# Expert matmuls over 240 instead of 256 token columns in a retention, mixture-of-experts and MLP kernel

## The chip, the core and the metric

The kernel runs on one core of one Trainium2 chip, as one program. The metric is the device time of an execution in microseconds (us); lower is better. Five engines work side by side and wait for each other through semaphores: TensorE (PE in the profile; its weight loads are listed apart as PEld), VectorE (DVE), ScalarE (ACT), GpSimd (POOL) and SyncE (SP), which here only issues DMAs. SBUF is the on-chip memory that the engines read; PSUM is the memory into which matmuls accumulate.

## What is computed

A retention layer (attention with a decay per head), then a layer of 8 experts in which each token goes to the one expert with the largest gate logit, then a dense two-layer MLP. Cut to the shapes and the parts that matter here:

```python
# q, k, v: (2, 8, 768, 64), lam: (8,)
x = attn(q, k, v, lam)                     # -> (1536 tokens, 512)

# experts: w_gate (512, 8), w1 (8, 512, 1024), w2 (8, 1024, 512)
logits = x @ w_gate
expert_idx = np.argmax(logits, axis=1)
gate_w = softmax(logits)[np.arange(N), expert_idx]
for e in range(E):
    mask = expert_idx == e
    h = np.maximum(x[mask] @ w1[e], 0.0)
    out[mask] = gate_w[mask, None] * (h @ w2[e])

# second MLP: w_in (512, 2048), w_out (2048, 512)
h = out @ w_in
return (h - np.tanh(h)) @ w_out
```

With the reference's own inputs the eight experts get 195, 205, 194, 205, 168, 157, 227 and 185 tokens, counted from `expert_idx`.

## The kernel before

The program has three stages, and PE goes through them in an order that is written out by hand.

**Attention and routing** (0 to about 97 us of the profile). Twelve tiles of 128 tokens. Matmuls here are plain float32 (type `F32`). Each tile's tokens are scaled by their gate and scattered by expert into rows of the DRAM tensor `xs_d`. `finish_routing` (line 485) counts the tokens of each expert and sets the flag `over` if a count is larger than `CAP` (256).

**Experts** (about 97 to 289 us). All matmuls of this stage are of type `F32R`, in which a matmul is one weight load and one matmul record. To keep float32's precision, each operand is split in a high and a low `F32R` part (`split`, lines 147 to 153: an ACT copy makes the high part at line 151, a DVE subtraction the low part at line 152), and each product is made of three matmuls: high by high, low by high, high by low. The stage has 64 steps n (8 experts by 8 blocks of 128 hidden columns, `EF` = 8). A step's `e_first` (lines 584 to 604) makes 12 matmuls with `w1` as the stationary operand and the tokens of the expert as the moving one, over `CAP` = 256 columns of tokens, whatever the expert's count is; ACT's Relu (line 602) and a DVE operation (line 603) turn the result into the two parts of `hb`. `e_second` (lines 608 to 629), two steps later, makes 12 matmuls with `w2` as the stationary and `hb` as the moving operand, again over 256 columns, and sums the 8 blocks in the two PSUM banks of `yp`. After an expert's last block ACT (line 627) and DVE (line 629) copy `yp` into `ysort`, from the column where the expert's tokens start; the columns beyond its count are overwritten by the next expert's copy.

In the same steps SP loads the weights ahead (`e_load1` for step n + 4, `e_load2` for step n + 2, 256 KB each) and, every second step, 512 KB of the second MLP's weights, which arrive as float64 and are turned into float32 by ACT, DVE and POOL (`decode_load`, `decode_math`, `decode_end`, lines 113 to 142). The two buffers `raw` of these loads are freed by the DVE operation at line 132, and SP, which issues in order, waits for that before it issues what stands behind. `x_trans` (line 524) turns the next expert's tokens once in 8 steps, with 8 transposes on PE.

**Second MLP** (about 289 us to the end). `m_first` (line 842) and `m_second` (line 922), all `F32R`, over windows of 512, 512, 256 and 256 tokens.

If `over` is set, a general path runs behind all of this (`window_table`, `window`): it takes the experts in windows of 256 tokens, and then the second MLP once more.

Of the kernel before, what the change touches and what calls it, by code (L numbers as in the profile page):

```python
# [13 lines left out]
ALU = mybir.AluOpType  # L14
# [1 line left out]
PSUM = bass.MemoryType.PSUM  # L16
DRAM = bass.MemoryType.DRAM

# (1 - tanh(s)/s)/s^2 with u = s^2 on 0 <= u <= T2, as Q4*((u+A1)^2+B1)*((u+A2)^2+B2)
T2 = 0.36  # L20
Q4 = 0.006269319839325208
A1, B1 = 0.64716093, 2.51604722 ** 2
A2, B2 = -2.33084468, 1.56360238 ** 2
# [4 lines left out]
def retention_moe_mlp(ctx: ExitStack, tc: tile.TileContext, q, k, v, lam, w_gate, w1, w2, w_in, w_out, out):  # L28
    nc = tc.nc
    pe, act, dve, pool, sp = nc.tensor, nc.scalar, nc.vector, nc.gpsimd, nc.sync  # L30
# [9 lines left out]
    EF = F // 128  # L40
    NF = FF // 128
    CAP = 256

    const = ctx.enter_context(tc.tile_pool(name="const", bufs=1))
    small = ctx.enter_context(tc.tile_pool(name="small", bufs=2))
# [4 lines left out]
    def slot(shape, dtype, name):  # L50
        return slp.tile(shape, dtype, tag="sl", name=name)

    def bank(shape, name):
        return ps.tile(shape, F32, tag="ps", name=name)

    def sm(shape, dtype, name):
        return small.tile(shape, dtype, tag=name, name=name)
# [30 lines left out]
    over = const.tile([128, 1], I32, name="over")  # L88
# [5 lines left out]
    biass = const.tile([128, 1], F32, name="biass")  # L94
    ysort = const.tile([128, KD, NT + CAP], F32, name="ysort")

# [10 lines left out]
    rev = at.tile([128, H], F32, name="rev")  # L107
    state = [at.tile([128, HP, 128], F32, name=f"state{b}") for b in range(B)]

# [1 line left out]
    dec = {}  # L111

    def decode_load(i):
# [60 lines left out]
    def e_split(n, which, new=slot):  # L174
        ews[n, which] = split(ewr.pop((n, which)), f"w{which}", new)

# [1 line left out]
    qkv = {}  # L178

    qrows, qts, qds = {}, {}, {}  # L180
# [281 lines left out]
    def setup_late():  # L462
# [6 lines left out]
        dve.tensor_copy(out=ebase_b, in_=ebase_i)  # L469
        pool.iota(slots_i, pattern=[[1, CAP]], base=1, channel_multiplier=0)  # L470
        dve.tensor_copy(out=slots, in_=slots_i)
# [9 lines left out]
    ebase_i = const.tile([128, E], I32, name="ebase_i")  # L481
    slots_both = slot([128, 2, CAP], F32, "slots")
    slots, slots_i = slots_both[:, 0, :], slots_both[:, 1, :].bitcast(I32)

    def finish_routing():
        tp = bank([128, E], "tp")
        pe.matmul(tp, lhsT=ones_b, rhs=cnt, start=True, stop=True)
        dve.tensor_copy(out=ct, in_=tp)
        inc = sm([128, E], F32, "inc")
        dve.tensor_tensor_scan(out=inc, data0=ones[:, 0:E], data1=ct, initial=0.0, op0=ALU.mult, op1=ALU.add)  # L490
        dve.tensor_tensor(out=starts, in0=inc, in1=ct, op=ALU.subtract)
        dve.tensor_copy(out=starts_i, in_=starts)
        cm = sm([128, 1], F32, "cm")
        dve.tensor_reduce(out=cm, in_=ct, axis=AX.X, op=ALU.max)
        dve.tensor_scalar(out=over, in0=cm, scalar1=float(CAP), scalar2=None, op0=ALU.is_gt)

    def token_table():
        dl = sm([128, E], F32, "dl")
# [11 lines left out]
        else:  # L510
            pool.dma_start(out=idx, in_=tok_d.rearrange("(t p) o -> p (t o)", p=128))

# [1 line left out]
    xrow, xhl = {}, {}  # L514

    def x_load(e):
# [7 lines left out]
    def x_trans(e):  # L524
        r = xrow.pop(e)
        hs, ls = [], []
        for g in range(2):
            xp = bank([128, 2, 2, 128], "xtp")
            for i in range(2):
                for j in range(2):  # L530
                    kk = 2 * g + i
                    pe.transpose(xp[:, i, j, :], r[j][:, kk * 128:(kk + 1) * 128], ident)  # L532
            hi = temp([128, 2, 256], F32R, "xh")
            act.copy(out=hi, in_=xp.rearrange("p i j c -> p i (j c)"))
            lo = temp([128, 2, 256], F32R, "xl")
            dve.tensor_tensor(out=lo, in0=xp.rearrange("p i j c -> p i (j c)"), in1=hi.bitcast(F32), op=ALU.subtract)
            hs.append(hi)
            ls.append(lo)
        xhl[e] = (hs, ls)
# [19 lines left out]
    def first_key(t):  # L559
        key = sm([128, 1], F32, "key")  # L560
        dve.scalar_tensor_tensor(out=key, in0=lgs[t][:, 1, 0:1], scalar=1.0, in1=ohs[:, t, 0:1], op0=ALU.add, op1=ALU.mult)
        perm = slot([128, CAP], F32, "perm")
        dve.tensor_scalar(out=perm, in0=slots, scalar1=key, scalar2=None, op0=ALU.is_equal)
# [17 lines left out]

    hhl = {}

    def e_first(*ns):
        tiles = []
        for n in ns:
            hs, ls = xhl[n // EF]
            ah, al = ews.pop((n, 1))
            tiles.append((n, hs, ls, ah, al, bank([128, CAP], "ehp")))
        for g in range(2):  # L590
            for n, hs, ls, ah, al, hp in tiles:
                for i in range(2):
                    kk = 2 * g + i
                    ks = slice(kk * 128, (kk + 1) * 128)
                    xh, xl = hs[g][:, i, :], ls[g][:, i, :]
                    pe.matmul(hp, lhsT=ah[:, ks], rhs=xh, start=(kk == 0), stop=False)  # L596
                    pe.matmul(hp, lhsT=al[:, ks], rhs=xh, start=False, stop=False)  # L597
                    pe.matmul(hp, lhsT=ah[:, ks], rhs=xl, start=False, stop=(kk == KD - 1))  # L598
        for n, hs, ls, ah, al, hp in tiles:
            hb = slot([128, 2, CAP], F32R, "hb")  # L600
            hh, hl = hb[:, 0, :], hb[:, 1, :]
            act.activation(out=hh, in_=hp, func=ACTF.Relu)
            dve.scalar_tensor_tensor(out=hl, in0=hp, scalar=0.0, in1=hh.bitcast(F32), op0=ALU.max, op1=ALU.subtract)
            hhl[n] = (hh, hl)

    ys = {}

    def e_second(n, col=None):
        e, f = divmod(n, EF)
        hh, hl = hhl.pop(n)  # L610
        bh, bl = ews.pop((n, 2))
        if f == 0:
            ys[e] = [bank([128, 2, CAP], "yp") for _ in range(2)]
        for g in range(2):
            for i in range(2):
                kk = 2 * g + i
                o = ys[e][g][:, i, :]
                wh = bh[:, kk * 128:(kk + 1) * 128]
                wl = bl[:, kk * 128:(kk + 1) * 128]
                for m, (a, b) in enumerate(((wh, hh), (wh, hl), (wl, hh))):  # L620
                    pe.matmul(o, lhsT=a, rhs=b, start=(f == 0 and i == 0 and m == 0), stop=(f == EF - 1 and m == 2),  # L621
                              skip_group_check=True)
        if f == EF - 1:
            yp = ys.pop(e)
            at_ = starts_i[0:1, e:e + 1] if col is None else col
            ra = act.value_load(at_, min_val=0, max_val=NT)
            act.copy(out=ysort[:, 0:2, bass.ds(ra, CAP)], in_=yp[0])
            rd = dve.value_load(at_, min_val=0, max_val=NT)
            dve.tensor_copy(out=ysort[:, 2:4, bass.ds(rd, CAP)], in_=yp[1])

# [1 line left out]
    whl = {}  # L632

    def m_split(i):
# [13 lines left out]

    ghl, outp = {}, {}

# [1 line left out]
    nd = [0]  # L652

    nl = [0]
# [117 lines left out]
    with tc.manual_schedule():  # L772
        NE = E * EF
        LAG = 2
        for n in range(NE + LAG):
            if n < NE:
                if n == 2:
                    finish_routing()
# [10 lines left out]
                if n == 0:  # L789
                    e_split(2, 1)  # L790
                    e_first(0, 1)
                elif n > 1:
                    e_first(n)
# [13 lines left out]
            if n >= LAG:  # L807
                e_second(n - LAG)
# [15 lines left out]
    o = 0  # L824
# [165 lines left out]
                g_high(w, fs)  # L990
                g_low(w, fs)

# [1 line left out]
    NWE = NT // CAP  # L994
    NWT = NWE + E

# [61 lines left out]
    def window(tab, t):  # L1058
        cur = tab[:, t, :]
        r = []  # L1060
        for i in range(2):
            a = slot([128, DM], F32, "xr")
            pool.indirect_dma_start(out=a, out_offset=None, in_=xs_d[:, :],
                                    in_offset=bass.IndirectOffsetOnAxis(ap=cur[:, i:i + 1].bitcast(U32), axis=0))
            r.append(a)
        er = sp.value_load(cur[0:1, 2:3], min_val=0, max_val=E - 1)
        xrow[0] = r
        x_trans(0)
        for f in range(EF):
            for g, ld in ((1, e_load1), (2, e_load2)):  # L1070
                ld(f, bass.ds(er, 1))
                e_split(f, g, temp)
            e_first(f)
            e_second(f, cur[0:1, 3:4])

    with tc.manual_schedule():
        second_mlp(True)
# [1 line left out]
    with tc.If(rv > 0):  # L1079
        with tc.manual_schedule():  # L1080
            tab = sm([128, NWT, 4], I32, "tab")
            window_table(tab)
            for t in range(NWT):
                window(tab, t)
            second_mlp(False)
# [30 lines left out]
```

## Time and profile before

| what | us |
|---|---|
| time, median of 3 runs | 570.04 |
| lowest and highest run | 569.59, 572.48 |
| span of the profiled execution, first to last instruction | 565.1 |
| PE matmuls busy in the span | 541.3 (96%) |
| PE weight loads busy | 486.8 (86%) |
| DVE, ACT, POOL busy | 451.8, 396.9, 115.6 |
| stage of the experts, about 97 to 289 us | 192 |

The profile shows one execution on the one core. Its span is 565.1 us; the time of a run is taken around the whole execution, and its median is 4.9 us above that span. Matmuls are pipelined: a record's duration (283 ns for 256 columns) is longer than the distance at which the next one starts, so the pace of a stream of matmuls is read from start times and not from durations. Views named below are the page's groups of instructions, the same grouping for one stretch or engine, the busy time by stretches, the chain of work that ended last, the order in time, and the waits.

### The profile page before, as it was taken

What the parts mean: (1) busy time and instruction counts of PE and PEld (TensorE: products, weight loads), DVE (VectorE), ACT (ScalarE), POOL (GpSimd) and SP (SyncE); (2) the same over time, 40 slices, a digit from 0 to 9 for tenths busy, and PEclk for the clock granted to TensorE, in tenths of its full rate; (3) what the DMA queues carried; (4) which work ended last, traced back from release to release, by engine and by line L of the source; (5) the groups of instructions that cost most, each with busy time, mean ns of one, the idle gap of its engine ahead of it and who ended that gap; (6) DMA issues with size and microseconds to landing.
All of it is one profiled execution on the core that took longest, in us unless ns stands there. A gap on an engine that the chain in (4) does not pass through costs nothing.

```text
span 565.1 us, 10631 instructions
## 1 busy us (share of the span) xinstructions
PE 541.3 (96%) x3901; PEld 486.8 (86%) x3901; DVE 451.8 (80%) x867; ACT 396.9 (70%) x752; POOL 115.6 (20%) x139
## 2 busy tenths in 40 slices
PE   6998889999999999999999999999999999999992
PEld 5877768999999999999988888888888889999982
DVE  5889896999888787888859989888676777777680
ACT  1454666878888888888669888777667576667561
POOL 3556443343443312211000000003000003001001
PEclk7899999999999999999999999999999999999997
DMA  6999867799999999898100000002000001001001
GB/s 144 265 317 304 201 189 219 258 244 298 291 291 317 277 306 292 270 312 251 38 0 1 1 2 0 1 0 77 1 1 0 1 1 75 1 0 39 1 1 42
DMA packets 93309, 75.26 MB, mean 133 GB/s; under 512 B 30272, under 2 KB 77376, under 8 KB 93248
## 3 DMA queue, kind: packets, MB, share of 16 engines
q1 hardware_dynamic: 90896, 68.19, 42.0%
q0 software_dynamic: 2352, 6.31, 3.1%
q8 instruction: 32, 0.52, 0.4%
q14 instruction: 29, 0.24, 0.1%
HBM read 63.99 MB, written 10.49 MB: 132 GB/s over the span
## 4 chain that ended last, share of the span: by engine, by line
PE 64%; issue 16%; DVE 11%; DMA 3%; ACT 3%; POOL 1%; SPq 1%; POOLq 0%; DVEq 0%
PE mhp L842 17%; PE outp L922 16%; PE yp L621 14%; PE ehp L597 5%; PE ehp L598 5%; PE ehp L596 5%; DVE at L288 2%; ACT qt L247 2%; DMA k<-in_k_dram 1%; DVE state L312 1%; DMA w2r<-in_moe_w_dram 1%; POOL out_dram L63 1%; DVE da L132 1%; DVE cnt L422 1%; PE xtp L532 1%
## 5 line engine op out<-in xcount | busy, mean ns | idle before, releaser
L621 PE MATMUL yp<-hb,w2h 128*128 128x256 f32 x512 | 95.3, 284 | 0.0
L842 PE MATMUL mhp<-yh,mh 128*128 128x512 f32 (+1 forms) x256 | 82.2, 337 | 0.6 <-ACT yh L151 0.6
L842 PE MATMUL mhp<-yh,ml 128*128 128x512 f32 (+1 forms) x256 | 81.9, 336 | 0.0
L621 PEld LDWEIGHTS yp<-hb,w2h 128*128 128x128 f32 x512 | 79.7, 192 | 0.0
L851 ACT ACTIVATE u<-mhp 128x512 f32<-128x512 f32 x48 | 28.7, 597 | 67.5 <-PE mhp L842 67.5
L597 PE MATMUL ehp<-xh,w1l 128*128 128x256 f32 x256 | 72.7, 284 | 0.6 <-DVE w1l L152 0.6
L596 PE MATMUL ehp<-xh,w1h 128*128 128x256 f32 x256 | 72.7, 284 | 0.0
L598 PE MATMUL ehp<-xl,w1h 128*128 128x256 f32 x256 | 72.4, 283 | 0.0
L621 PE MATMUL yp<-hb,w2l 128*128 128x256 f32 x256 | 72.4, 283 | 0.0
L63 POOL DMA_INDIRECT out_dram<-ysort,idx x12 | 13.0, 1082 | 280.3 <-ACT ysort L927 278.2
L873 DVE SCALAR_TENSOR_TENSOR s<-s,u 128x512 f32<-128x512 f32 x48 | 33.1, 690 | 44.2 <-ACT s L853 44.2
L141 POOL TENSOR_TENSOR dw<-da,sg 128x512 f32<-128x512 f32 x32 | 43.5, 1360 | 112.0 <-ACT da L140 84.5
L922 PE MATMUL outp<-ml,gh 128*128 128x512 f32 x192 | 56.0, 392 | 0.0
L922 PE MATMUL outp<-mh,gh 128*128 128x512 f32 x192 | 56.0, 392 | 0.0
L922 PE MATMUL outp<-mh,gl 128*128 128x512 f32 x192 | 55.5, 391 | 0.0
L842 PE MATMUL mhp<-yl,mh 128*128 128x512 f32 (+1 forms) x256 | 54.8, 336 | 0.0
L842 PEld LDWEIGHTS mhp<-yh,mh 128*128 128x128 f32 x256 | 48.2, 188 | 7.1 <-ACT yh L151 1.5
L842 PEld LDWEIGHTS mhp<-yh,ml 128*128 128x128 f32 x256 | 48.2, 188 | 5.5
L597 PEld LDWEIGHTS ehp<-xh,w1l 128*128 128x128 f32 x256 | 49.1, 192 | 1.3 <-DVE w1l L152 1.2
L152 DVE TENSOR_TENSOR w1l<-w1r,w1h 128x512 fp32r<-128x512 f32 x64 | 46.3, 724 | 3.8 <-ACT w1h L151 0.7
L596 PEld LDWEIGHTS ehp<-xh,w1h 128*128 128x128 f32 x256 | 49.1, 192 | 0.0
L598 PEld LDWEIGHTS ehp<-xl,w1h 128*128 128x128 f32 x256 | 49.1, 192 | 0.0
(147 smaller groups left out, 1269.3 us busy)
## 6 DMA issues: line engine op xcount, KB each, us to landing
w1r<-in_moe_w_dram SPq DMA_DIRECT2D x64, 256.0 KB, 5.6
w2r<-in_moe_w_dram SPq DMA_DIRECT2D x64, 256.0 KB, 5.7
raw<-in_moe_w_in_dram SPq DMA_DIRECT2D x16, 512.0 KB, 5.6
raw<-in_moe_w_out_dram SPq DMA_DIRECT2D x16, 512.0 KB, 5.3
xs_d<-zrow SPq DMA_DIRECT2D x16, 256.0 KB, 4.8
xr<-xs_d SPq DMA_DIRECT2D x16, 256.0 KB, 6.3
q<-in_q_dram SPq DMA_DIRECT2D x12, 256.0 KB, 4.7
v<-in_v_dram SPq DMA_DIRECT2D x12, 256.0 KB, 5.3
```

The costliest lines, as they stand in the source:

```text
L63: ins = pool.indirect_dma_start(out=dst[:, :], out_offset=bass.IndirectOffsetOnAxis(ap=ix.bitcast(U32), axis=0), in_=src, in_offset=None)
L141: pool.tensor_tensor(out=w, in0=a.bitcast(F32), in1=sg, op=ALU.mult)
L152: dve.tensor_tensor(out=lo, in0=src, in1=hi.bitcast(F32), op=ALU.subtract)
L247: act.copy(out=o, in_=src)
L596: pe.matmul(hp, lhsT=ah[:, ks], rhs=xh, start=(kk == 0), stop=False)
L597: pe.matmul(hp, lhsT=al[:, ks], rhs=xh, start=False, stop=False)
L598: pe.matmul(hp, lhsT=ah[:, ks], rhs=xl, start=False, stop=(kk == KD - 1))
L621: pe.matmul(o, lhsT=a, rhs=b, start=(f == 0 and i == 0 and m == 0), stop=(f == EF - 1 and m == 2), skip_group_check=True)
L842: pe.matmul(hp[:, j, :], lhsT=a[:, sl], rhs=b, start=(i == 0), stop=(i == 3 * KD - 1))
L851: act.activation(out=u, in_=hp, func=ACTF.Square)
L873: dve.scalar_tensor_tensor(out=s1, in0=s1, scalar=B1, in1=u, op0=ALU.add, op1=ALU.mult)
L922: pe.matmul(outp[w][i], lhsT=a[:, sl], rhs=b, start=(fs[j] == 0 and m == 0), stop=done)
```

## The change

A constant `WT = 240` is added, and the normal path uses it as the width of an expert: the moving operands of both layers' matmuls, the PSUM tile of `e_first`, the Relu and the DVE operation behind it, the matmuls of `e_second` and the two copies into `ysort`. `over` is now set if an expert has more than 240 tokens. The general path passes 256 as width and stays as it is. Loads, transposes, splits of weights and tokens, and the order of all work are the same.

```diff
+    WT = 240
...
-        dve.tensor_scalar(out=over, in0=cm, scalar1=float(CAP), scalar2=None, op0=ALU.is_gt)
+        dve.tensor_scalar(out=over, in0=cm, scalar1=float(WT), scalar2=None, op0=ALU.is_gt)
...
-    def e_first(*ns):
+    def e_first(*ns, wd=WT):
...
-            tiles.append((n, hs, ls, ah, al, bank([128, CAP], "ehp")))
+            tiles.append((n, hs, ls, ah, al, bank([128, wd], "ehp")))
...
-                    xh, xl = hs[g][:, i, :], ls[g][:, i, :]
+                    xh, xl = hs[g][:, i, 0:wd], ls[g][:, i, 0:wd]
...
-            hh, hl = hb[:, 0, :], hb[:, 1, :]
+            hh, hl = hb[:, 0, 0:wd], hb[:, 1, 0:wd]
...
-    def e_second(n, col=None):
+    def e_second(n, col=None, wd=WT):
...
-                o = ys[e][g][:, i, :]
+                o = ys[e][g][:, i, 0:wd]
...
-            act.copy(out=ysort[:, 0:2, bass.ds(ra, CAP)], in_=yp[0])
+            act.copy(out=ysort[:, 0:2, bass.ds(ra, wd)], in_=yp[0][:, :, 0:wd])
...
-            dve.tensor_copy(out=ysort[:, 2:4, bass.ds(rd, CAP)], in_=yp[1])
+            dve.tensor_copy(out=ysort[:, 2:4, bass.ds(rd, wd)], in_=yp[1][:, :, 0:wd])
...
-            e_first(f)
-            e_second(f, cur[0:1, 3:4])
+            e_first(f, wd=CAP)
+            e_second(f, cur[0:1, 3:4], wd=CAP)
```

## Rows read from the trace of the kernel before

**Rows 1.** Page, groups: line, engine, out<-in, shape, count | busy us, mean ns | idle.
```profile
L621 PE MATMUL yp<-hb,w2h 128*128 128x256 f32 x512 | 95.3, 284 | 0.0
...
L597 PE MATMUL ehp<-xh,w1l 128*128 128x256 f32 x256 | 72.7, 284 | 0.6 <-DVE w1l L152 0.6
...
L621 PE MATMUL yp<-hb,w2l 128*128 128x256 f32 x256 | 72.4, 283 | 0.0
```

**Rows 2.** Busy us (and count) of each engine by stretches of the experts' stage.
```profile
core 0: us, PE busy (x) PEld busy (x) DVE busy (x) ACT busy (x) POOL busy (x), PEclk, DMA share, GB/s
97.00:125.00 28.00, 27.73 (x229) 27.28 (x228) 26.77 (x50) 23.58 (x47) 9.83 (x10) 1.00 0.85 251
125.00:150.00 25.00, 24.64 (x206) 24.44 (x205) 22.31 (x39) 20.93 (x41) 11.72 (x13) 1.00 1.05 297
150.00:200.00 50.00, 50.00 (x421) 50.00 (x420) 41.66 (x75) 43.35 (x84) 17.98 (x20) 1.00 1.02 298
200.00:250.00 50.00, 50.00 (x421) 50.00 (x420) 40.65 (x74) 42.33 (x82) 12.04 (x9) 1.00 0.91 288
250.00:289.00 39.00, 39.00 (x326) 38.80 (x325) 31.78 (x55) 28.20 (x58) 3.09 (x3) 1.00 0.46 142
```

**Rows 3.** Waits of the weight loads, 97 to 289 us: us, times, longest.
```profile
PEld ehp L597 <- DVE w1l L152: 1.2, 3, 0.6
```

**Rows 4.** Chain that ended last, by time: start us, us, what; 256 columns.
```profile
156.54 0.87 PE xtp L532 x8
...
160.28 1.44 PE yp L621 x12
...
163.16 1.44 PE yp L621 x12
```

**Rows 5.** Order in time on PE: start us, us, what; 512 columns, second MLP.
```profile
294.50 1.07 PE L842 MATMUL mhp<-yl,mh 128*128 128x512 f32 x4
...
297.22 1.07 PE L842 MATMUL mhp<-yl,mh 128*128 128x512 f32 x4
```

**Rows 6.** Order in time, weight loads: start us, us, what; matmuls of 8 columns.
```profile
89.82 0.97 PEld L364 LDWEIGHTS lr<-wg,xt 128*128 128x128 f32 x8
```

**Rows 7.** Groups of weight loads by form: busy us, mean ns of one.
```profile
L621 PEld LDWEIGHTS yp<-hb,w2h 128*128 128x128 f32 x512 | 79.7, 192 | 0.0
...
L364 PEld LDWEIGHTS lr<-wg,xt 128*128 128x128 f32 x8 | 1.0, 191 | 0.1
```

**Rows 8.** Groups on ACT and DVE, 97 to 289 us.
```profile
L151 ACT CAST w1h<-w1r 128x512 fp32r<-128x512 f32 x62 | 38.0, 613 | 1.2 <-DMA w1r<-in_moe_w_dram 1.2
L602 ACT ACTIVATE hb<-ehp 128x256 fp32r<-128x256 f32 x64 | 24.5, 383 | 26.7 <-PE ehp L598 25.6 <-PE tp L487 0.3
...
L603 DVE SCALAR_TENSOR_TENSOR hb<-ehp,hb 128x256 fp32r<-128x256 f32 x64 | 26.8, 420 | 19.7 <-ACT hb L602 19.5
L132 DVE SCALAR_TENSOR_TENSOR da<-raw,da 128x512 int32<-128x512 int32 x27 | 18.7, 692 | 0.9
```

**Rows 9.** Busy time behind the experts' stage, columns as in the stages' view.
```profile
289.00:565.10 276.10, 265.50 (x1345) 225.97 (x1344) 209.26 (x326) 191.44 (x329) 14.02 (x23) 0.99 0.03 12
```

**Rows 10.** Busy time in a stretch of the second MLP, columns as in the stages' view.
```profile
400.00:500.00 100.00, 100.00 (x524) 86.04 (x523) 73.39 (x114) 66.41 (x114) 4.69 (x8) 1.00 0.03 11
```

**Rows 11.** Page, slices of 14.1 us: GB/s that the DMAs moved.
```profile
GB/s 144 265 317 304 201 189 219 258 244 298 291 291 317 277 306 292 270 312 251 38 0 1 1 2 0 1 0 77 1 1 0 1 1 75 1 0 39 1 1 42
```

**Rows 12.** Landing times of the loads at line 163, 120:180, then 180:260.
```profile
DMA to landing us min/median/max: 6.0/7.3/8.6
...
DMA to landing us min/median/max: 3.6/5.4/6.7
```

**Rows 13.** SP's own waits, 100 to 290 us.
```profile
SPq L118 <- DVE da L132: 33.4, 12, 3.3
```

**Rows 14.** Line 569, plain float32, 256 columns: duration ns min/median/max, first and last start us.
```profile
L569 PE MATMUL xtp<-perm,xg x16: 379/379/462, 93.5 to 96.8; 128*128 128x256 f32 x16
```

## The prediction

> **What bounds the kernel now.** I read the page's groups first, to see how much of PE's time the change can reach. The five groups of the experts' matmuls hold 512 + 4 x 256 = 1536 matmuls of 256 columns (three of the five stand there; those of lines 596 and 598 are like that of 597) [rows 1]. All of them get 16 columns fewer, and no other matmul does.
>
> Then I read the busy time by stretches, because an average over the span mixes stages. In the experts' stage PE is busy 50.00 of 50 us from 150 to 250 us and 39.00 of 39 us behind that, while DVE has 41 to 42 us of 50 and ACT 42 to 43 [rows 2]. Busy time alone doesn't show that PE sets the pace, since records overlap. The waits do: over the whole stage the weight loads waited only 1.2 us in three places, all for the DVE part of a `w1` split [rows 3]. One stretch is different: from 97 to 125 us DVE is busy 26.77 of 28 us, 96% [rows 2]. There the splits of the first steps and what is left of the routing are queued on DVE, and PE is just behind it.
>
> So from about 125 us the order on PE is the clock of this stage, and the question is what one matmul costs there. Durations (283 ns) don't tell it; distances of starts do. In the chain the `yp` group of one step starts at 160.28 us and that of the next at 163.16; 24 matmuls lie between, so one takes 2.88 / 24 = 0.1200 us [rows 4]. At 512 columns, in the second MLP, a group starts at 294.50 and the next like it at 297.22, with 12 matmuls between: 2.72 / 12 = 0.2267 us [rows 5]. Both are `F32R`, each with its own weight load, at the full granted clock (1.00, the 2.4 GHz level [rows 2]).
>
> **The change part by part.** The two paces give a line: (226.7 - 120.0) / 256 = 0.417 ns a column, and 120.0 - 256 x 0.417 = 13.3 ns that don't depend on columns. At 240 columns this is 13.3 + 100.0 = 113.3 ns, 6.67 ns less. For 1536 matmuls: 1536 x 6.67 = 10.2 us, if every one lies on the path and nothing else holds the pace at 120.
>
> No row shows an `F32R` matmul of fewer than 256 columns, so the pace at 240 is bounded by neighbours. From below: eight matmuls of 8 columns, whose weights are 128 x 128 too, start their weight loads at (0.97 - 0.19) / 7 = 0.111 us from each other [rows 6, 7]. With 8 columns that can't be the moving operand, so a weight load by itself allows about 111 ns. The line's 113.3 stands just above that, so at 240 columns the columns still decide, by 2 ns; the gain can't be much more than 10.2 us in any case. From above: the pace stays at 120 and the gain is zero. I take 113.3, since two measured points with the same operand type lie on that line and the weight-load limit lies under it.
>
> Off PE's path, the Relu and the DVE operation behind `e_first` and the copies to `ysort` get shorter. Relu takes 383 ns for 256 columns and a cast of 512 takes 613 [rows 8], 0.9 ns a column, so 14 ns each; the DVE operation 420 against 692 for 512 [rows 8], 1.06 ns a column, so 17 ns each. These run beside PE, which hides them; only in the DVE-bound stretch do some ten of them count, 0.2 us. The last expert's copies lie on the path into the second MLP, and lose 32 columns: 0.03 us. The changed comparison for `over` is the same instruction with another constant. Strides: `hb`, `xh` and `yp` keep their layout, so a matmul reads and writes 240 columns in a row as it did 256.
>
> What of the 10.2 us doesn't arrive? From 97 to 125 us DVE sets the pace. PE has 229 instructions there [rows 2], 229 x 6.67 ns = 1.5 us, which PE will spend waiting for the splits; the 0.2 us of DVE comes back. Then the other engines have to follow a faster PE. A pair of steps takes 5.76 us of matmuls now and 5.44 then, 5.6% less. ACT rises from 87% (43.35 of 50) to 92% and DVE from 83% to 88%, neither full.
>
> The sum is 10.2 - 1.5 = 8.7 us. Against the profiled execution's span of 565.1 us that makes 556.4 us, and with the 4.9 us between this span and the median of the runs, 561.3 us. Behind the stage nothing changes: the 276 us of the second MLP [rows 9] begin earlier, with all of its weights loaded.
>
> **The rivals.** *Weight loads hold the pace at 120 (570.0 us).* The weight-load records fill 50.00 of 50 us in the experts' stage [rows 2], against 86 of 100 in the second MLP [rows 10], where the columns clearly decide. If the 13.3 ns belong to the exchange of weights and come on top of a load of 106.7, the pace is 120 at any width up to 256, and the two points of the line can't tell that apart, because 256 columns at 0.417 ns are 106.7 too. Then the time is 570.0. Against it: the weight loads of the 8-column matmuls have the same record length (191 against 192 ns [rows 7]) and come at 111, not 120. Those are plain float32 and not `F32R`, which leaves it open. The Trainium skill, in "Perfetto Trace Analysis", section "Identifying the Most-Contended Engine", judges PE's headroom by the weight loads' busy share rather than by that of the matmuls; by that rule the stage with its full share has nothing to give, and the time would be that of this rival. The trace agrees with it only as far as the share, since these records (192 ns at a distance of 120) overlap each other.
>
> *Loads don't follow (568.0 us).* From 125 to 200 us the DMA share is over 1.0 at 297 to 298 GB/s [rows 2]. A pair of steps loads 1664 KB (two `w1`, two `w2`, one `raw`, a quarter of an expert's tokens) in 5.98 us with its share of the transposes (0.87 us in 8 steps [rows 4]), 285 GB/s; at 5.66 us it needs 301. If the DMAs can't give it, nothing is gained until the last `raw`, at about 250 us: some 1000 matmuls, 6.7 us, are lost of the 8.7. Against it: two slices inside the stage moved 317 and 312 GB/s [rows 11], and the landing time of `w1` fell from 7.3 to 5.4 us at the same pace of PE [rows 12], so the supply was catching up. SP also waits mostly for DVE to free `raw` (33.4 us at line 118, and as often at line 122) [rows 13], that is for work that moves with PE.
>
> *The narrow matmul falls to the rate of plain float32 (1019 us).* This is the one on the slower side. PE has two rates for four-byte operands: 0.417 ns a column for `F32R` on the line above, and at line 569 for plain float32 sixteen records for eight matmuls of 256 columns, (96.8 - 93.5) / 15 = 0.22 us each [rows 14], 0.44 us a matmul, about four times as much. Every `F32R` matmul of this trace has 256 columns or 512. If the fast rate is bound to a width of at least 256, each of the 1536 takes 240 / 256 x 0.44 = 0.41 us, 0.29 more than now: 449 us, so 1019 us. If only one record at 0.206 is made of it, 132 us, so 702 us. The point from which it decides is whether 240 columns still count as wide enough. Nothing in the trace speaks for such a bound, and nothing excludes it: no narrower one was run.
>
> *The guard sends the kernel on the general path.* The largest expert has 227 tokens by the reference, so `over` stays zero. If it didn't, 14 windows of 8 steps at 2.88 us and a second MLP of 276 us [rows 4, 9] would be added, about 1170 us.
>
> **How the numbers follow.** Forecast, 561.3 us: 0.52. Weight loads hold the pace, 570.0: 0.19. Loads don't follow, 568.0: 0.08. Rate of plain float32, 1019 (702 at the least): 0.20. General path: 0.01. The forecast's own range is 558.8 (all 10.2 us arrive and the run is like the fastest of before, a little below) to 566 (half of it lost to loads). The range over the cases is 558.8 to 572.5: it takes in no change at the slowest run of before and leaves out the two slow cases, 0.21. About 0.5% (2.9 us) is what a measurement of this kernel can tell from no change. Faster by more than that: 0.52, the forecast. Within it: 0.19 + 0.08 = 0.27. Slower: 0.21.
>
> **What would show it.** Right: in the chain, `yp` groups of neighbouring steps 2.72 us apart instead of 2.88 (113.3 ns a matmul), the stage from the first `ehp` to the last `yp` some 8.7 us shorter, waits for `w1` splits before 125 us a little longer, and the second MLP unchanged at 276 us. Weight loads as the bound: `ehp` and `yp` still 2.88 apart, with shorter records. Loads as the bound: steps at 2.72 where no `raw` is loaded, longer ones with waits for `w1` or `w2` before 250 us. The slow rate: twice as many records in these groups, or the same number at 0.2 us or more from each other. The prediction is wrong above all if the pace at 240 columns isn't on the line through 256 and 512.

## The result: 565.9 us, 0.8% faster, about half of what the sum gave

| | median | lowest to highest | runs |
|---|---|---|---|
| before | 570.51 us | 567.36 to 577.89 | 16 |
| 240 columns | 565.86 us | 563.83 to 568.90 | 16 |

The ratio is 0.9919, with a 95% interval of 0.9901 to 0.9937: 4.6 us faster, clear of zero, where the sum said 8.7. The profiled executions show less still, 563.9 against 565.1 us of span. The profiled run of the changed kernel took 565.62 us with a span of 563.9, so a time is 1.7 us above its span and not 4.9; the profile of before, with its 565.1, was then an execution of about 566.8 us, faster than any of its 16 timed runs. It showed the kernel before at its best, without waits that its ordinary runs may have. Lines of the changed kernel stand one higher than before (line 621 is 622).

Page, groups, of the changed kernel, which answer to [rows 1] (columns as there):

```profile
L622 PE MATMUL yp<-hb,w2h 128*128 128x240 f32 x512 | 90.9, 278 | 0.0
...
L598 PE MATMUL ehp<-xh,w1l 128*128 128x240 f32 x256 | 70.9, 277 | 1.2 <-DVE w1l L153 1.1
```

The counts are the same: one record for each matmul of 240 columns. Busy time by stretches, which answers to [rows 2], the last line to [rows 9]:

```profile
core 0: us, PE busy (x) PEld busy (x) DVE busy (x) ACT busy (x) POOL busy (x), PEclk, DMA share, GB/s
97.00:125.00 28.00, 27.15 (x237) 26.63 (x236) 26.82 (x50) 23.56 (x47) 9.98 (x11) 1.00 0.84 246
125.00:150.00 25.00, 23.50 (x206) 22.93 (x205) 21.00 (x38) 20.20 (x39) 10.11 (x11) 1.00 1.01 278
150.00:200.00 50.00, 45.42 (x385) 44.56 (x384) 39.60 (x70) 40.23 (x78) 19.98 (x23) 0.97 0.98 280
200.00:250.00 50.00, 50.00 (x450) 50.00 (x449) 43.59 (x80) 45.00 (x89) 11.92 (x9) 1.00 0.99 311
250.00:286.50 36.50, 36.48 (x326) 36.29 (x325) 31.36 (x55) 27.81 (x58) 3.41 (x3) 1.00 0.51 159
286.50:563.90 277.40, 265.73 (x1344) 226.19 (x1344) 209.44 (x326) 191.41 (x329) 13.99 (x23) 0.99 0.03 12
```

Read the counts: from 200 to 250 us PE ran 450 instructions where it ran 421, 7% more. From 150 to 200 us it ran 385, fewer than before, and was idle for 4.6 us, while the DMAs were busy all the time (0.98) at 280 GB/s, less than the 298 of before. What it waited for stands in the waits of PE from 97 to 289 us (engine, line, waited for: us, times, longest) and in the chain that ended last (start us, us, what), here from 149 to 187 us:

```profile
PE xtp L533 <- DMA xr<-xs_d: 5.7, 4, 3.6
```

```profile
149.39 7.52 DMA xr<-xs_d
156.95 0.98 PE xtp L533 x7
157.93 1.34 PE yp L622 x12
160.61 1.34 PE yp L622 x12
...
165.97 1.34 PE yp L622 x12
...
172.57 10.33 DMA xr<-xs_d
182.95 1.86 PE xtp L533 x8
184.81 2.33 PE yp L622 x12
```

Two things are to be seen. Where nothing waits, two steps take 165.97 - 160.61 = 5.36 us, 111.7 ns a matmul: better than the 113.3 of the sum. And the chain leaves PE for the loads of the next expert's tokens (`xr`): the load issued at 172.57 took 10.3 us to land, where the loads of tokens landed within 6.9 us in the kernel before, and PE stood still for 3.6 us before the transposes. Behind that stop the clock was down. By stretches, the granted clock (behind the five engines) is 0.54 from 184 to 187 us, near the lower of the two levels, 1.2 GHz, and the twelve `yp` matmuls at 184.81 took 2.33 us instead of 1.34:

```profile
180.00:184.00 4.00, 1.05 (x6) 0.96 (x7) 2.74 (x5) 2.67 (x6) 0.77 (x2) 0.92 1.04 338
184.00:187.00 3.00, 3.00 (x17) 3.00 (x16) 2.55 (x4) 2.54 (x5) 0.33 (x1) 0.54 1.15 246
187.00:200.00 13.00, 13.00 (x119) 13.00 (x118) 8.94 (x18) 9.89 (x20) 4.70 (x4) 1.00 0.87 266
```

The other loss lies at the start of the second MLP. Chain of the changed kernel:

```profile
285.85 0.57 ACT ysort L628
286.42 0.02 issue
286.44 0.63 ACT yh L152
...
287.70 0.68 DVE yl L153
288.39 0.58 DVE ysort L630
288.97 0.02 issue
288.99 0.63 ACT yh L152
289.62 0.04 issue
289.66 5.38 PE mhp L843 x22
```

The last copy into `ysort` on DVE (line 630) stands behind two `yl` operations, and the third and fourth `yh` wait for that copy; in the kernel before the copy stands ahead of all four. The copy belongs to the experts' hand-ordered region, the `yl` operations to that of the second MLP. Within a region the order is the program's; across the border of the two it came out differently at 240 columns, which no line of the diff asks for. (The text ahead of the prediction says that the order of all work is the same; at this place it isn't.) PE waited 1.3 us in one place there, and the part behind the last `yp` is 277.4 us instead of 276.1.

So the profiled execution adds up. From the first `ehp` to the last `yp` it took 189.8 us instead of 192.2: 1536 matmuls at 111.9 instead of 119.9 ns (means from 200 to 250 us) are 12.3 us less; the stops before three groups of transposes gave back 1.7, 1.3 and 4.5 us (by start times, beyond what the same place takes without a wait), the lower clock 1 us more, and what is left, 1.4 us, falls mostly to the DVE-bound first part (0.9 us by its counts, below). Then 1.3 us were lost at the start of the second MLP.

### The profile page after: what moved, and what is told of

Read it like the earlier page. It is cut to its first block, busy times and chain, and to the rows that moved or that the text cites. A ratio compares the mean times of both kernels' runs of the same rounds, so it can differ in the third digit from the quotient of the medians.

```text
span 563.9 us, 10632 instructions
## 1 busy us (share of the span) xinstructions
PE 532.3 (94%) x3901; PEld 476.9 (85%) x3901; DVE 450.1 (80%) x867; ACT 395.3 (70%) x752; POOL 116.3 (21%) x139
## 4 chain that ended last, share of the span: by engine, by line
PE 61%; issue 16%; DVE 10%; DMA 6%; ACT 3%; POOL 1%; SPq 1%; POOLq 0%; DVEq 0%
PE mhp L843 16%; PE outp L923 15%; PE yp L622 13%; DMA xr<-xs_d 5%; PE ehp L598 4%; PE ehp L599 4%; PE ehp L597 4%; DVE at L289 2%; ACT qt L248 2%; DMA k<-in_k_dram 1%; POOL out_dram L64 1%; PE xtp L533 1%; DVE state L313 1%; DVE cs L387 1%; DVE cnt L423 1%
## 5 line engine op out<-in xcount | busy, mean ns | idle before, releaser
L622 PE MATMUL yp<-hb,w2h 128*128 128x240 f32 x512 | 90.9, 278 | 0.0
L622 PEld LDWEIGHTS yp<-hb,w2h 128*128 128x128 f32 x512 | 78.1, 192 | 0.0
L598 PE MATMUL ehp<-xh,w1l 128*128 128x240 f32 x256 | 70.9, 277 | 1.2 <-DVE w1l L153 1.1
L622 PE MATMUL yp<-hb,w2l 128*128 128x240 f32 x256 | 70.9, 277 | 0.0
L597 PE MATMUL ehp<-xh,w1h 128*128 128x240 f32 x256 | 70.6, 276 | 0.0
L599 PE MATMUL ehp<-xl,w1h 128*128 128x240 f32 x256 | 70.5, 275 | 0.0
L153 DVE TENSOR_TENSOR w2l<-w2r,w2h 128x512 fp32r<-128x512 f32 x64 | 48.3, 754 | 1.9 <-ACT w2h L152 1.3
L622 PEld LDWEIGHTS yp<-hb,w2l 128*128 128x128 f32 x256 | 48.9, 191 | 0.1
```

The costliest lines, as they stand in the source:

```text
L153: dve.tensor_tensor(out=lo, in0=src, in1=hi.bitcast(F32), op=ALU.subtract)
```

## Experiments

The theory: the pace of PE is as forecast or better, and the missing microseconds are the waits for loads, which have a cause in the DMAs between 125 and 190 us, and the order on DVE. The rivals: only the tokens' load is issued too late; or another engine holds PE; or the kernel's time doesn't depend on either. Each kernel of this section ran beside the kernel before on the same chip. The ratio given is the recorded one with its 95% interval; it isn't the quotient of the two medians, and differs from that by up to 0.4 points. The names in brackets are those that the quoted expectations use.

**Order on DVE** (order_240). The split of the first window of `ysort` into `yh` and `yl`, `y_split(0)`, is called at the end of the experts' region instead of at the start of the next one; the list of windows that it needs is made earlier for that:

```diff
...
             decode_flush()
+        y_split(0)
...
-        y_split(0)
+        if not fresh:
+            y_split(0)
```

> The changed kernel at 240 columns, with the split of the first window's ysort moved into the hand-ordered region of the experts, so that on DVE the last copy into ysort stands ahead of the four yl operations, as it did in the kernel before. In the changed kernel two of the four yl operations stand ahead of that copy, and PE waits 1.5 us at the start of the second MLP. Theory (that wait is on the path): about 1.4 us faster than the changed kernel, 564.5 us, or 0.9895 of the kernel before. Rival (it only moves a wait that comes anyway): the same as the changed kernel, 565.9 us, 0.992.

Measured: 0.9880 (0.9842 to 0.9918) of the kernel before, 561.1 us against 567.6 on that chip. The chain has lost the detour:

```profile
278.04 3.36 PE yp L622 x30
281.40 0.02 issue
281.43 0.57 ACT ysort L628
282.00 0.02 issue
282.02 0.63 ACT yh L152
282.64 0.04 issue
282.69 7.53 PE mhp L844 x31
```

What lies behind the last `yp` is 276.9 us, near the 276.1 of before, where the kernels of 228 to 248 columns with the other order have 277.4 to 279.3. The place of the wait is shown by the chain; the gain in time, 0.4 points of the ratio, is no larger than the intervals (they overlap with that of the changed kernel).

**Tokens earlier** (x_early_240, x_early_256). From the third expert on, the load of an expert's tokens is issued two steps earlier, into buffers of another pool that are free by then, at 240 and at 256 columns:

```diff
-            a = temp([128, DM], F32, "xr")
+            a = slot([128, DM], F32, "xr")
...
-                if n % EF == 1 and n // EF + 1 < E:
-                    x_load(n // EF + 1)
+                if n == 1:
+                    x_load(1)
+                if n % EF == 7 and n // EF + 2 < E:
+                    x_load(n // EF + 2)
```

> The changed kernel at 240 columns, with the load of the next expert's tokens issued two steps earlier, into buffers of the large pool instead of the small one. Theory A (the part of the gain that is missing went into transposes that wait for these loads: 1.7, 1.3 and 4.5 us in the profiled run): 3 to 6 us faster than the changed kernel, 560 to 563 us, 0.982 to 0.987 of the kernel before, and no wait of PE for the tokens in the profile. Theory B (the DMAs as a whole don't deliver enough between 125 and 200 us, and the tokens are only what shows it): the waits move to the splits of w1 and w2, and the time stays within 1.5 us of the changed kernel, 564.5 to 566 us.

> Control: the same earlier load of tokens in the kernel before, at 256 columns. If the tokens' lateness belongs to the narrower matmuls alone, no change: 570.5 us, 1.000. If ordinary runs of the kernel before already lose time to it (its profiled run, with a span of 565.1 us, shows no such wait, but its runs lie between 567 and 578), some 1 to 3 us faster: 567.5 to 569.5, 0.995 to 0.998.

Measured: 0.9932 (0.9904 to 0.9960) at 240 columns, no better than the changed kernel, and 0.9975 (0.9953 to 0.9997) at 256. Theory B holds. The waits of PE from 97 to 289 us at 240 columns have changed their name, and the stretch from 125 to 200 us still moves 277 GB/s with the DMAs fully busy:

```profile
PE ehp L598 <- DVE w1l L153: 4.2, 12, 0.7
```
```profile
125.00:200.00 75.00, 72.15 (x609) 69.26 (x608) 59.90 (x107) 60.38 (x118) 29.39 (x33) 1.00 1.01 277
```

No wait for tokens is left; instead twelve matmuls wait for splits of `w1`, whose loads land late: from 120 to 190 us they take 8.3 us in the median from issue to landing, and 7.2 in the kernel before. The lateness is of the loads as a whole. (The early tokens also hold buffers of the pool in which `w1` and `w2` land; what that costs by itself was not tested, but at 256 columns the same edit brought one such wait of 0.3 us.) The control suggests that the timed runs of the kernel before lose a little to it too, 1.4 us, with an interval from 0.2 to 2.7.

**Fewer bytes** (half_raw_240). The raw weights of the second MLP are loaded by half from the ninth load on:

```diff
-            sp.dma_start(out=r, in_=src)
+            ks = slice(0, KD if i < 8 else KD // 2)
+            sp.dma_start(out=r[:, ks], in_=src[:, ks])
```

The first edit is that for `w_in`; `w_out` has the same.

> The changed kernel at 240 columns, with the loads of the second MLP's raw weights from the ninth on cut to half: 256 instead of 512 KB each, 1408 instead of 1664 KB in two steps; the second MLP computes with old values in the other half, and every other instruction stays. Theory (the missing gain is lost to loads that don't arrive in time): no wait of PE for loads behind 130 us, the steps at 2.69 us throughout, the experts' stage 181 to 183 us instead of 189.8, and 557 to 560 us by the measure in which the changed kernel takes 565.9, 0.977 to 0.983 of the kernel before. Rival (what is missing is lost to DVE, ACT or the order of work): within 1.5 us of the changed kernel.

Measured: 0.9883 (0.9840 to 0.9925), some 2 us better than the changed kernel, with intervals that overlap, and not the 6 to 9 of the theory. In the profiled execution the experts' stage is 185.9 us, 3.9 us shorter than that of the changed kernel. A miss, and the useful one. With 15% fewer bytes the DMAs are as busy as before from 125 to 200 us, but move less; from 200 us on they move more at a lower share:

```profile
125.00:200.00 75.00, 71.91 (x623) 71.18 (x622) 64.90 (x113) 63.58 (x124) 29.74 (x33) 0.98 0.97 253
...
200.00:250.00 50.00, 50.00 (x450) 50.00 (x449) 43.63 (x80) 44.94 (x89) 12.60 (x9) 1.00 0.84 262
```

PE still waited for tokens that took up to 8.5 us to land. At full pace these steps would need 1408 KB in 5.36 + 0.22 us, 258 GB/s. So bytes are a part of what fills the DMAs here, and not all of it: something else in that stretch does too, which is gone by 200 us. From there on the changed kernel, with all its bytes, moves 311 GB/s at a share of 0.99.

**Scatters later** (order_tok_late_240). One thing ends at that time: the twelve scatters of token numbers into `tok_d` (POOL, 512 B each in 4-byte pieces), which stand in every second step from 6 to 28, and the read of the result in step 30. Nothing needs them before the second MLP writes its first output rows. Moved to steps 36 to 58, the read to step 60 (the expectation names 32 and 62, two steps more), with the order on DVE put right as above:

```diff
-                if n >= 6 and n % 2 == 0 and n < 6 + 2 * (NTT + 1):
-                    token_scatter((n - 6) // 2)
+                if n >= 36 and n % 2 == 0 and n < 36 + 2 * (NTT + 1):
+                    token_scatter((n - 36) // 2)
```

> order_240 with the twelve small scatters of token numbers (POOL, 512 B each in 4-byte pieces) moved from steps 6 to 32 to steps 36 to 62 of the experts' stage. In all kernels so far the DMAs moved 275 to 298 GB/s from 125 to 200 us and up to 323 behind that, and the scatters end at about 187 us. Theory A (the scatters hold the DMAs back): from 125 to 200 us 300 GB/s and more, PE's waits for the tokens' loads (4.5 us in order_240) gone, and 3 to 5 us faster than order_240: 0.979 to 0.983 of the kernel before; the lower rate then shows from 200 to 260 us. Theory B (they have no part in it): the waits and the rates stay, 0.988.

Measured: 0.9810 (0.9780 to 0.9840), 556.2 us against 568.2; each of its six runs is faster than each of the six of order_240. Theory A holds, in time and in the rows that it named. Its stretches:

```profile
125.00:150.00 25.00, 24.14 (x216) 23.95 (x215) 22.31 (x41) 21.77 (x43) 5.66 (x5) 1.00 1.02 323
150.00:200.00 50.00, 50.00 (x450) 50.00 (x449) 43.57 (x79) 45.10 (x89) 13.25 (x11) 1.00 0.98 307
200.00:250.00 50.00, 50.00 (x450) 50.00 (x450) 43.66 (x78) 43.74 (x87) 23.47 (x27) 1.00 1.05 291
```

PE is busy without a gap from 150 us, with 450 instructions in 50 us in both stretches. The rate is 307 to 323 GB/s where the scatters were, and 291 where they are now. A pace of 301 GB/s was what the sum needed, and 305 at the measured 5.36 us for a pair of steps. Take all kernels that load all bytes, and of their stretches from 125 to 150, 150 to 200 and 200 to 250 us those with a share of 0.97 or more: where the scatters run through most of the stretch, 274 to 298 GB/s were moved; where at most one falls in, 305 to 324. That POOL is merely kept from other work isn't the reason: from 97 to 289 us of the changed kernel, SP waited for POOL once, for 0.4 us, and no other engine did. The loads of tokens tell the same, from issue to landing, in this kernel, first from 125 to 187 us and then from 187 to 250:

```profile
DMA to landing us min/median/max: 5.0/5.1/6.1
...
DMA to landing us min/median/max: 5.5/6.8/7.5
```

In the kernel before the same two stretches have it the other way round, 6.3/6.5/6.9 and then 4.9/5.6/6.2. In this execution the slower loads from 200 us on cost nothing; that 70 us without scatters had given them a lead is the likely reason, but no run tests it. The experts' stage is 181.6 us, 10.6 less than before: the 12.3 us of the pace less what the DVE-bound first part keeps.

The two controls, the later scatters alone at 256 and at 240 columns (tok_late_256, tok_late_240):

> Control: the scatters of token numbers moved to steps 36 to 62 in the kernel before, at 256 columns. Theory (the scatters slow the loads, but at 120 ns a matmul the loads mostly keep up all the same): at most what the earlier load of tokens gave there, 0.995 to 1.000 of the kernel before. Rival (the scatters cost as much at 256 columns, and the late scatters are a gain of their own): 0.990 or less.

> The changed kernel with only the scatters moved, the order on DVE at the start of the second MLP as the changed kernel has it. If the late scatters and the order are two separate costs of the changed kernel: 0.984 of the kernel before, between order_tok_late_240 (0.981) and the changed kernel (0.992), with the 1.5 us wait of PE at the start of the second MLP still there. If the order costs nothing once the loads keep up: 0.981.

Measured: 0.9967 (0.9939 to 0.9994) at 256 columns and 0.9829 (0.9782 to 0.9876) at 240. At 256 the scatters cost little, 1.9 us, as the first theory said; at 240 moving them gives 0.9 points, some 5 us. The rate falls with them at 256 too, and there it isn't for want of demand, since the share rises. The stretches from 150 to 200 us, without scatters, and from 200 to 250, with them:

```profile
150.00:200.00 50.00, 50.00 (x420) 50.00 (x420) 40.95 (x74) 42.43 (x82) 11.60 (x9) 1.00 0.92 291
200.00:250.00 50.00, 50.00 (x420) 49.95 (x419) 41.16 (x74) 42.79 (x83) 21.80 (x27) 1.00 1.00 276
```

With the scatters out of the way in both, the narrower matmuls are worth 0.9967 - 0.9829, 1.4% or 7.8 us; the medians of the two, on the same chip, are 6.7 us apart (566.5 and 559.8). In the profile at 240 the start of the second MLP still has its wait of 1.3 us, so order and scatters show as two separate waits; the times don't separate them, since 0.9829 and 0.9810 overlap in their intervals. And the later place isn't free in every execution: in this one PE waited for loads again between 219 and 258 us, 1.7 us in all, and ran 436 instead of 450 instructions from 200 to 250 us.

**Scatters last** (order_tok_last_240). One scatter a step in steps 50 to 61, the read in step 62:

```diff
-                if n >= 36 and n % 2 == 0 and n < 36 + 2 * (NTT + 1):
-                    token_scatter((n - 36) // 2)
+                if 50 <= n < 50 + NTT + 1:
+                    token_scatter(n - 50)
```

> order_tok_late_240 with the scatters of token numbers put into steps 50 to 62, one in each, where hardly any raw weights are loaded. Theory (scatters cost only where the loads have no slack): no wait of PE for loads behind 130 us in any run, 312 GB/s and more from 125 to 200 us and 300 and more from 200 to 245, and 0.977 to 0.981 of the kernel before. Rival (the scatters in steps 36 to 62 had cover enough): 0.981, like order_tok_late_240.

Measured: 0.9812 (0.9787 to 0.9837). No further gain, so the rival holds: in time, the steps from 36 on were cover enough.

**The pace by width** (w228, w248, w128). What sets the pace of 111.9 ns at 240 columns? The changed kernel with another width, 228, 248 or 128; for 128 columns the flag `over` is left at `CAP`, and the tokens beyond an expert's first 128 are left out:

```diff
-    WT = 240
+    WT = 228
```

> The changed kernel with 228 instead of 240 columns (the largest expert has 227 tokens). Theory A (columns set the pace, 13.3 ns + 0.417 ns a column): 108.3 ns a matmul against the 112 measured at 240, 5.7 us less in the sum of 1536, so 560 to 563 us with some of it lost to waits. Theory B (at 240 the weight load already sets the pace, 111 to 112 ns): the pace stays at 111 to 112 ns, and the time at that of the changed kernel, 565 to 566 us.

> The changed kernel with 248 columns, for the pace alone, read between 200 and 250 us. On the line of 256 and 512 columns: 13.3 + 103.3 = 116.7 ns. If the pace falls to that of the weight loads as soon as the width is under 256: 112.

> The changed kernel with 128 instead of 240 columns, the guard left at 256; tokens of an expert beyond its first 128 are left out. For the pace alone, read between 200 and 250 us. If the weight load is the limit that 240 columns already touch: 111 to 112 ns a matmul, one record each, as at 240. If the columns still counted: 13.3 + 53.3 = 67 ns. If a narrow matmul fell to the rate of plain float32: two records each, or 200 ns and more.

The time at 228 columns was 0.9915 (0.9878 to 0.9952), that of the changed kernel; 248 and 128 were run once, for the pace alone. For the pace, neighbouring `yp` groups of the chain, 24 matmuls apart; 228, 248 and 128 columns:

```profile
212.73 1.34 PE yp L622 x12
215.41 1.34 PE yp L622 x12
```
```profile
204.93 1.38 PE yp L622 x12
207.69 1.38 PE yp L622 x12
```
```profile
208.03 1.34 PE yp L622 x12
210.71 1.34 PE yp L622 x12
```

That is 2.68 / 24 = 111.7 ns at 228, 2.76 / 24 = 115.0 at 248 and 111.7 at 128; 240 has 111.7 as well, and 256 has 120.0 [rows 4]. From 240 columns down, the columns have no part in it. What is left is the weight load, at the 111 ns that the matmuls of 8 columns gave [rows 6], or else a fixed cost of any matmul. A fixed cost it isn't. In the kernel before, two `bf16` matmuls of 8 columns, each with a weight load of 128 x 128 of its own, start 0.04 us apart (start us, us, what):

```profile
90.92 0.18 PE L413 MATMUL lr<-cnt,ones_b 128*128 128x8 bf16 x1
90.96 0.17 PE L414 MATMUL lr<-ohs,tri 128*128 128x8 bf16 x1
```

So the weight load of four-byte operands is the reading that fits all of these rows; no run changed that load by itself. At 248, columns still count, and the line of 256 and 512 (116.7 there) is 1.7 ns too high. The narrow matmul doesn't fall to the rate of plain float32; the number of records is the same.

## Why the prediction was right, and where its steps were off

It was right in direction, and the time lies in the range and just inside the forecast's own (565.9 of at most 566), where half of the gain is lost to loads. The sum itself, 561.3, was not met: the pace gave more than it says, the loads and the order on DVE took more, and that the two left the time inside is in part luck. By its steps:

- *PE sets the pace, and 16 columns fewer shorten it.* Right: 450 instead of 421 instructions in 50 us.
- *113.3 ns by the line, the columns deciding by 2 ns.* The term was mis-sized: 111.9 ns, and 12.3 us instead of 10.2. The bound from below, 111 ns from the 8-column matmuls, was nearly the value itself, and the columns decide nothing at 240; 228 and 128 columns show it.
- *1.5 us lost in the DVE-bound stretch.* Right in kind, 0.9 in size: from 97 to 125 us PE ran 237 instead of 229 instructions, which is 0.9 us gained of some 1.8 at the measured pace; DVE is at 96% as before, and PE's idle time there rose from 0.3 to 0.9 us.
- *The loads follow.* This step failed, and "Loads don't follow" was its rival, given 0.08. The mechanism was only half that rival's: not what the DMAs can give at all, since 323 GB/s were moved in the same stretch once the scatters were gone, but what they give while the scatters run, 274 to 298 GB/s over stretches of 25 and 50 us, below the 301 that the narrower steps need. Taking away half of the raw bytes gave back some 2 us; moving 6 KB of scatters gave back 4 to 5. The argument against the rival took two slices of 14 us, 317 and 312 GB/s [rows 11], for a rate that holds on. The first (170 to 184 us) has two scatters in it, so a short stretch can move more than 298 beside them; the second (240 to 254 us) has none. And the fall of the landing time, read as the supply catching up [rows 12], came with the end of the scatters at 187 us: with the scatters moved, the loads of tokens landed faster early and slower late.
- *Waits for the loads would be for `w1` or `w2`.* It was the tokens. PE uses them three steps after their load is issued, and `w1` and `w2` four. With the tokens early it was `w1`.
- *Behind the stage nothing changes.* Failed by 1.3 us, by an order of instructions on DVE that the diff doesn't show.
- *Weight loads hold the pace at 120 (0.19).* Wrong at that value; right in that there is a bound which doesn't depend on columns, at 112 ns, reached from 240 columns down. The Trainium skill, in "Perfetto Trace Analysis", section "Identifying the Most-Contended Engine", judges PE's headroom by the weight loads' busy share, beside the share of peak arithmetic. Here the measurement differs: at 256 columns the weight loads' share was full (50.00 of 50 us [rows 2]), and at 240 columns 7% more instructions ran in the same time (450 against 421).
- *Rate of plain float32 (0.20).* Excluded at 248, 240, 228 and 128 columns: one record for each matmul, 111.7 to 115.0 ns apart.
- *4.9 us between span and time.* Wrong: 1.7 us. The two numbers belong to different executions: the profile of before was of an unusually good one, without waits that ordinary runs may have.

Not settled: why scatters of 512 B in 4-byte pieces slow the large loads. It isn't the time of the scatters' own packets: from 150 to 187 us of the changed kernel these took 0.4% of the DMA engines' time, and those of SP's queue 101.3%. The packets in the traces show what changes: a few of SP's packets get very long, and the rest stay as they are. From 130 to 185 us, 165 of 15917 packets of the changed kernel took over 400 ns, 16% of all packet time; with the scatters moved (order_tok_late_240) it was 48 of 17434, 3%. From 202 to 245 us it is the other way round, 5% and 13%. The median packet of 2 KB took 84 ns with the scatters and 89 without. What stalls the long ones is open.

## What to carry to other kernels

A step that makes the bounding engine faster is worth what its suppliers can follow; look for the stretch where the DMAs are already at a share of 1.0, and ask what else is in their queues there and whether it must be there. The kernel at 240 columns with the token scatters 30 steps later and the split of the first window in the experts' region took 0.981 of the kernel before, against 0.992 for the change alone. And compare the order of instructions on each engine after a change of a size alone: where two hand-ordered regions meet, the scheduler may choose anew.

## What the runs showed of the hardware that was not expected

- A stream of `F32R` matmuls with a weight load each costs 111.7 ns a matmul at 128, 228 and 240 columns, 115.0 at 248 and 120.0 at 256; under 240 columns nothing is gained.
- While twelve scatters run that move 6 KB in all, the DMAs move 274 to 298 GB/s, and 305 to 324 without them, at a share of busy time of 0.97 to 1.05 in both; the difference sits in some 1% of the packets, which take over 400 ns.
- At 128 columns PE waited for tokens at about 130 us, its clock fell to the lower level, and it stayed there although PE was busy without a gap: 176 instructions in the 37 us from 133 us on, at a granted clock of 0.50, where the 22 us from 178 us on had 194. With about half the columns the one run took 578.8 us. At 240 columns the clock was back at 1.00 from 187 us on, after the stop that ended at 183. By stretches, at 128 columns:

```profile
133.00:170.00 37.00, 37.00 (x176) 37.00 (x174) 15.63 (x30) 16.60 (x35) 9.44 (x12) 0.50 0.68 207
178.00:200.00 22.00, 21.60 (x194) 21.41 (x194) 15.66 (x32) 17.20 (x36) 9.72 (x13) 1.00 0.80 222
```
